# A forward and backward pass of four layers on one core: direct weight transposes, and layer inputs and query pairs transposed by DMA

## The chip, the cores and the metric

The kernel runs on one core of a Trainium2 chip. The engines named here are TensorE (PE, with PEld for its weight loads), VectorE (DVE), ScalarE (ACT), GpSimd (POOL) and SyncE (SP, which issues nearly all DMAs, in its program order). The metric is the device time of one execution, in microseconds (us); the kernel before was timed in three runs.

## The reference

A sequence of 2048 rows of width 512 passes through four residual layers: linear attention A, gated unit B, A, B, with the same weights in both A layers and in both B layers. The kernel returns the output and the gradients with respect to the input and the five weight matrices, all in bf16.

```
def A(x):    # 32 heads of 16, phi(t) = where(t > 0, t + 1, exp(t)) + 1e-6
    q, k, v = heads(x @ wqkv);  pq, pk = phi(q), phi(k)
    kv = pk^T v  (per head);    z = sum over the rows of pk
    return ((pq kv) / (pq . z + 1e-6)) @ wo
def B(x):    # F = 1376
    return (sigmoid(x @ w_gate) * (x @ w_up)) @ w_down
x = x + A(layernorm(x));  x = x + B(layernorm(x))
x = x + A(layernorm(x));  x = x + B(layernorm(x))
out, vjp = jax.vjp(...);  grads = vjp(grad_out)
```

## The kernel before, in words

The 2048 rows are 16 tiles of 128 rows (index `st`, `NST` = 16). The layers are numbered `l` = 0 (A), 1 (B), 2 (A), 3 (B). F = 1376 is taken in three slices (512, 512, 352) and in 11 chunks of 128, the last of which has 96 rows (`FLAST`).

The stages, in order: `kq_fwd` of layer 0 (keys and queries of all tiles, to 60 us); `ab_fwd` of layers 0 and 1 (60 to 205 us), which is called the lower pass here; `kq_fwd` of layer 2 (to 255); `ab_fwd` of layers 2 and 3 (to 395), the upper pass; then the backward pass, `b_bwd_p1` of layer 3, `a_bwd_p1` of layer 2, `b_bwd_p1` of layer 1, `a_bwd_p1` of layer 0. Units of weight gradient (`W.run(n)`, L1495 and L1511) are run between the steps of the backward pass and by themselves where the next step has nothing to do yet; `HOLD` = 6 of them are kept back for the start of `b_bwd_p1` of layer 1.

In these stages PE, ACT, DVE and POOL run in the order in which the program is written. The order of the DMAs on SP is found by the scheduler; `tc.issue_after(x)` only says that a DMA comes after `x`. At most eight DMAs of the queue are under way; each waits for the one issued eight before it.

One tile of an `ab_fwd` pass does the attention part of a tile ahead and the gated unit of tile `st`:

- the "front" of a tile ahead, `FLAG` = 3 tiles: `prod` (POOL, L840), `front1` (DVE, the sum over a head, L846), `front2` (DVE, add and reciprocal L850 and L851, and the multiplication that gives the normalised queries `pqn`, L863), and `front3` (four PE transposes of 128 x 128 to `pqnT`, L374, copied out by ACT);
- `attn_y` of tile `st + 2` (`YLAG`): four matmuls (L884), the residual added on DVE (L892), and the statistics of the next layernorm (DVE and POOL, L449 to L455); `ln.apply` (ACT, L460) makes the normalised input `hstage`, and `ln.stage_T` transposes it to `hT` with four PE transposes (L374) and an ACT copy (L383);
- `gu` for the three slices: g and u products on PE (L922), sigmoids on ACT (L924, L926), `hh_t` on DVE (L929, which releases the bank of u) and `ssd_t` on POOL (L930). PSUM has two banks each for g and u and one for y;
- `hh_t` transposed to `hhT`, by DMA in tiles 2 to 14 (`dma_T`, L949), and `finish` (11 matmuls with w_down, L956) of an earlier tile; tile 3 has no `finish`, so it is shorter. In the lower pass the statistics of the following layernorm come on DVE too.

The backward pass of B needs the three B weights transposed: `wdT`, `wuT`, `wgT`. `wT_units` makes them in the lower pass, piece by piece: a DMA transpose from the input into a staging tile (L404, L406, L420) and a store to DRAM (L409, L412, L421). From there they are loaded whole (L201, L206, L208): in the upper pass after tiles 2, 5 and 8, and by `load_b_weights` at the start of `b_bwd_p1` of layer 1. Of the last chunk of `wuT` and `wgT` only 96 rows are loaded; the transposes of `dd` and the matmuls of `dh` (L1252) take 96 rows there.

`kq_fwd` of layer 0 takes its tiles `a_t` from three buffers; each is stored (`sv_phq`, L642) before it is used again.

Of the kernel before, what the change touches and what calls it, by code (L numbers as in the profile page):

```python
# [60 lines left out]
def kernel(  # L61
# [42 lines left out]
    for l in range(4):  # L104
# [17 lines left out]
    k.wT = dict(  # L122
        wgT=dram.tile([NFC * P, D], BF16, name="wgT_d"),
        wuT=dram.tile([NFC * P, D], BF16, name="wuT_d"),
        wdT=dram.tile([D, F], BF16, name="wdT_d"),
    )
# [12 lines left out]
    with tc.tile_pool(name="wfwd", bufs=1, reuse_waits="tile") as wfwd, ExitStack() as lctx, tc.manual_schedule(engines=EM):  # L139
# [44 lines left out]
        with tc.tile_pool(name="aq0", bufs=1, reuse_waits="tile") as aq:  # L184
            A = kq_fwd(k, aq, 0, lns[0], lns[1], x_bf)
            with tc.tile_pool(name="wt_stage", bufs=2, reuse_waits="tile") as wt_stage:
                piece, flush = wT_units(k, wt_stage, B_w_gate, B_w_up, B_w_down)
                piece()
                piece()
                A.tail()  # L190
                ab_fwd(k, A, lns[1], {**{st: piece for st in range(0, 14, 2)}, NST - 2: flush}, nxt=lns[2])
        xctx.close()
        with tc.tile_pool(name="aq2", bufs=1, reuse_waits="tile") as aq:
# [4 lines left out]
            def b_weight_loads():  # L198
                def wd():
                    k.wdT = wb.tile([P, NDC, F], BF16, name="wdT", tag="w_c")  # L200
                    nc.sync.dma_start(out=k.wdT[:], in_=k.wT["wdT"].rearrange("(c p) f -> p c f", p=P))  # L201

                def wx(nm, tag):
                    t = wb.tile([P, NFC, D], BF16, name=nm, tag=tag)
                    setattr(k, nm, t)
                    nc.sync.dma_start(out=t[:, 0:NFC - 1, :],  # L206
                                      in_=k.wT[nm][0:(NFC - 1) * P, :].rearrange("(c p) j -> p c j", p=P))
                    nc.sync.dma_start(out=t[0:FLAST, NFC - 1, :], in_=k.wT[nm][(NFC - 1) * P:F, :])  # L208
                return wd, lambda: wx("wuT", "w_a"), lambda: wx("wgT", "w_b")
# [20 lines left out]
            def last_cb(i):  # L230
                if i == 0:
                    k.pre["gT"] = pre.tile([P, NDC, P], BF16, name="pre_gT")
                    g_transposes(k, k.pre["g"][:, 0, :], k.pre["gT"])
                else:
                    k.pre["dd"] = pre.tile([P, 2, F], BF16, name="pre_dd")
                    for fs in range(2):
                        dd_ops(k, k.pre["dd"], k.pre["ssd"], fs, dhh_mm(k, k.pre["gT"], fs))
            A.tail()
            ab_fwd(k, A, lns[3], dict(zip((2, 5, 8), b_weight_loads())), out_cb=out_cb, last_cb=last_cb)
# [5 lines left out]
    if True:  # L245
        def load_b_weights():
            wd, wu, wg = b_weight_loads()
            wd()
            wu()
            with tc.issue_after(k.hold):  # L250
                wg()
# [10 lines left out]
        k.load_b_weights, k.load_a_weights = load_b_weights, load_a_weights  # L262
# [55 lines left out]
        a_bwd_p1(k, R, 2, W, mk_out_cb=mk_gbf_cb)  # L318
        W.run(W.left() - HOLD)
# [76 lines left out]
def wT_units(k, stage, B_w_gate, B_w_up, B_w_down):  # L396
    nc = k.nc
    units, stores = [], []

    def by_rows(src, c0, n, dst):  # L400
        def unit():
            t = stage.tile([P, NDC, D], BF16, name="wt_st")
            nfull = min(n, F // P - c0) if src.shape[-1] == F else n
            nc.sync.dma_start(out=t[:, 0:nfull, :], in_=src[:, c0 * P:(c0 + nfull) * P], transpose=True)  # L404
            if nfull < n:
                nc.sync.dma_start(out=t[:, nfull, :], in_=src[:, F - P:F], transpose=True)  # L406

            def store():
                nc.sync.dma_start(out=dst[c0 * P:(c0 + nfull) * P, :].rearrange("(n p) d -> p n d", p=P),  # L409
                                  in_=t[:, 0:nfull, :])  # L410
                if nfull < n:
                    nc.sync.dma_start(out=dst[(c0 + nfull) * P:F, :], in_=t[P - FLAST:P, nfull, :])  # L412
            stores.append(store)
        return unit

    def by_cols(src, f0, w, dst):
        def unit():
            t = stage.tile([P, NDC, D], BF16, name="wt_st")
            v = t[:].rearrange("p a b -> p (a b)")[:, 0:NDC * w].rearrange("p (a b) -> p a b", a=NDC)
            nc.sync.dma_start(out=v, in_=src[f0:f0 + w, :], transpose=True)  # L420
            stores.append(lambda: nc.sync.dma_start(  # L421
                out=dst.rearrange("(c p) f -> p c f", p=P)[:, :, f0:f0 + w], in_=v))
        return unit

    for f0, w in FSL:
        units.append(by_cols(B_w_down, f0, w, k.wT["wdT"]))
    for src, nm in ((B_w_up, "wuT"), (B_w_gate, "wgT")):
        for c0, n in ((0, 4), (4, 4), (8, 3)):
            units.append(by_rows(src, c0, n, k.wT[nm]))

    def flush():
        for store in stores:
            store()
        stores.clear()

    def piece():
        old = stores[:]
        stores.clear()
        units.pop(0)()
        for store in old:  # L440
            store()
    return piece, flush


# [18 lines left out]
class FwdLN:  # L463
# [25 lines left out]
    def stage_T(self, st, evac="vector"):  # L489
# [6 lines left out]
        self.hTs[st] = hT  # L496

# [59 lines left out]
def kq_fwd(k, aq, l, ln, ln_next, x_src=None):  # L557
# [10 lines left out]
    with ExitStack() as ctx:  # L568
# [91 lines left out]
        def qa_tiles():  # L660
            if l == 0:
                return (work.tile([P, 2, D], BF16, name="e_t", bufs=2)[:, 1, :],
                        work.tile([P, 2, D], BF16, name="a_t", bufs=3)[:, 1, :])
# [30 lines left out]
        for st in range(NST):  # L694
# [4 lines left out]
            if l == 0:  # L699
                e_t = work.tile([P, 2, D], BF16, name="e_t", bufs=2)  # L700
                a_t = work.tile([P, 2, D], BF16, name="a_t", bufs=3)
# [123 lines left out]
YLAG = 2  # L825
FP = NFC * P
HH_DMA = {1: range(2, NST - 1), 3: range(2, NST - 1)}


def attn_fronts(k, A, pool, small):  # L830
# [23 lines left out]
    def front2(st):  # L854
# [11 lines left out]
        if st % 2 == 1:  # L866
            nc.sync.dma_start(out=dram_batch(sva["pqn"], st // 2, 2), in_=cur["pqn"][:])

    def front3(st, bank="ln", evac="scalar"):
        if st >= NST:  # L870
            return
        f = F_[st]
        pqnT = pool.tile([P, NDC, P], BF16, name="pqnT", bufs=3)
# [29 lines left out]
def ab_fwd(k, A, ln, side, nxt=None, out_cb=None, last_cb=None):  # L903
# [3 lines left out]
    with ExitStack() as ctx:  # L907
# [4 lines left out]

        by_dma = HH_DMA[l]

# [59 lines left out]
        for st in range(NST):  # L974
# [6 lines left out]
            if st in by_dma:  # L981
                nc.gpsimd.memset(T["hh"][:, F:FP], 0.0)
                A.front1(st + FLAG)
                A.front2(st + FLAG)
                gu(T, hT, 0)
                A.attn_y(st + YLAG)
                A.prod(st + 1 + FLAG)
# [4 lines left out]
                ln.stage_T(st + 1, "scalar")  # L992
                gu(T, hT, 2)
            elif st == 0:
# [40 lines left out]
            if st > 0:  # L1035
                ln.apply(st + YLAG)
                if st == 1:
# [116 lines left out]
def b_bwd_p1(k, l, W, mid):  # L1154
# [3 lines left out]
    if not first:  # L1158
        k.load_b_weights()
    with ExitStack() as ctx:  # L1160
# [39 lines left out]
        def transposes(T, fs):  # L1200
            dd, ddT = T["dd"], T["ddT"]
            fcs = fchunks_of_slice(fs)
            nfull = len([fc for fc in fcs if fc_rows(fc) == P])
            tps = ps_tile(k, "t", [P, 2, 4, P], BF16, "T_ps")
            for a in range(2):
                src = dd_part(dd, a, fs)
                for i, fc in enumerate(fcs):
                    r = fc_rows(fc)
                    nc.tensor.transpose(tps[0:r, a, i, :], src[:, i * P:i * P + r], k.ident[:])  # L1209
            out = ddT[:, 2 * fcs[0]:2 * (fcs[-1] + 1), :].rearrange("p (a n) t -> p a n t", a=2)  # L1210
            nc.scalar.copy(out[:, :, 0:nfull, :], tps[:, :, 0:nfull, :])  # L1211
            if nfull < len(fcs):
                nc.scalar.copy(out[0:FLAST, :, nfull, :], tps[0:FLAST, :, nfull, :])
# [32 lines left out]
        def dh_mm(T, lo, hi):  # L1246
            if lo == 0:
                T["dh"] = ps_tile(k, "y", [P, D], F32, "dh_ps")
            for i in range(lo, hi):
                a, fc = divmod(i, NFC)  # L1250
                r = fc_rows(fc)
                nc.tensor.matmul(T["dh"][:], lhsT=T["ddT"][0:r, dd_block(a, fc), :], rhs=(k.wuT, k.wgT)[a][0:r, fc, :],  # L1252
# [653 lines left out]
```

## Time and profile before

| | us |
|---|---|
| median of 3 runs | 1133.44 (1133.23 to 1135.18) |
| the profiled execution | 1135.02 |
| its span, from the first to the last instruction | 1133.3 |
| PE busy in the span | 1109.4 |
| DVE, ACT, POOL busy | 706.9, 484.2, 291.2 |
| PE busy in the lower pass, 60 to 205 us | 138.5 of 145 |
| PE busy in the upper pass, 255 to 395 us | 134.8 of 140 |

A busy time is the time in which an engine had an instruction under way. A timeline line gives the start, the time taken, the engine, the line of the kernel, the operation, the tile written and the tiles read, and in brackets how long the engine had been idle and what ended that. For a DMA, "to landing" is the time from the start of its issue on SP to its arrival. The DMA share is the mean busy share of the 16 DMA engines; packets that overlap in one engine can bring it over 1.

### The profile page before, as it was taken

Reading aid. Unit: us, or ns where it says so; the run is one execution under the profiler, and the core shown is the slowest. Engines: PE = TensorE matmul, PEld = TensorE weight load, DVE = VectorE, ACT = ScalarE, POOL = GpSimd, SP = SyncE. Lnnn points to the kernel's source line nnn. Section 1 sums busy time; section 2 is a strip of 40 time slices with the busy share of each in tenths; the row PEclk is TensorE's granted clock in tenths of the full one; section 3 lists DMA queues with packets and bytes.
Section 4 is the critical chain, followed back from the end, with each engine's and each line's share of the span. In section 5 each row is a group of like instructions: output and inputs, shape, how many; then the busy total and the mean of one; then the engine's idle time right before and its main releaser. Section 6 shows DMA issues by size and latency. Waiting matters only on the chain.

```text
span 1133.3 us, 20011 instructions
## 1 busy us (share of the span) xinstructions
PE 1109.4 (98%) x7468; PEld 648.8 (57%) x7468; DVE 706.9 (62%) x1344; ACT 484.2 (43%) x909; POOL 291.2 (26%) x518
## 2 busy tenths in 40 slices
PE   8979999998999999999999999999999999999998
PEld 4444554444555555554456468855546745448888
DVE  6788886778776456664975850166664976852211
ACT  6676666555756543433625431224324515410000
POOL 5647776435666400000110220000000110210000
PEclk9999999999999999999999999999999999999999
DMA  8967999855899999997899997799998899969996
GB/s 270 309 197 212 273 282 283 245 142 183 223 294 265 269 261 262 302 255 207 222 244 313 220 260 237 195 283 289 257 283 260 205 282 289 241 194 298 263 205 192
DMA packets 413682, 282.36 MB, mean 249 GB/s; under 512 B 198608, under 2 KB 399504, under 8 KB 409744
## 3 DMA queue, kind: packets, MB, share of 16 engines
q1 hardware_dynamic: 412432, 280.03, 90.3%
q8 instruction: 58, 0.95, 0.3%
q10 hardware_dynamic: 1152, 1.05, 0.3%
q14 instruction: 40, 0.33, 0.1%
HBM read 125.44 MB, written 115.70 MB: 213 GB/s over the span
## 4 chain that ended last, share of the span: by engine, by line
PE 89%; DVE 6%; DMA 3%; ACT 1%; issue 1%; POOL 0%; DVEq 0%; SPq 0%; POOLq 0%
PE p_ps L1511 18%; PE dh_ps L1252 13%; PE dh_ps L1756 7%; PE p_ps L1495 7%; PE y_ps L956 6%; PE dhh_ps L1110 6%; PE g_ps L922 6%; PE u_ps L922 6%; PE T_ps L1209 3%; PE dpk_ps L1791 2%; PE GT_ps L1652 2%; PE dp_ps L1624 2%; PE y_ps L884 2%; PE t_mm L616 2%; PE X_ps L624 2%; PE t_ps L374 1%
## 5 line engine op out<-in xcount | busy, mean ns | idle before, releaser
L1511 PE MATMUL p_ps<-p_set,p_a 128*128 128x256 bf16 (+1 forms) x2032 | 210.1, 264 | 0.0
L1511 PEld LDWEIGHTS <-p_a 128*128 128x128 bf16 x2048 | 185.9, 98 | 22.2
L1132 DVE TENSOR_TENSOR dd<-dhh_ps,ssd 128x512 bf16<-128x512 f32 x144 | 82.4, 629 | 121.3 <-PE dhh_ps L1110 117.4
L930 POOL TENSOR_TENSOR ssd_t<-hh_t,oms 128x512 bf16<-128x512 bf16 (+1 forms) x96 | 100.7, 1060 | 50.1 <-ACT out_t L226 13.5
L1252 PEld LDWEIGHTS <-ddT 128*128 128x128 bf16 (+1 forms) x704 | 67.6, 98 | 74.6 <-DMA ddT<-dd 2.4
L922 PEld LDWEIGHTS <-hT 128*128 128x128 bf16 x768 | 72.5, 98 | 65.2 <-DVE hT L381 1.4
L1084 POOL TENSOR_SCALAR ab<-c 128x2 f32<-128x2 f32 x64 | 12.4, 194 | 377.9 <-DVE junk L1081 364.7
L1211 ACT COPY ddT<-T_ps 128x1024 bf16<-128x1024 bf16 (+1 forms) x72 | 58.8, 819 | 115.2 <-PE T_ps L1209 62.0
L1076 ACT ACTIVATE t_sb<-dh_ps,rstd_all 128x512 f32<-128x512 f32 x64 | 44.0, 688 | 115.7 <-issue 65.0
L922 PE MATMUL g_ps<-wg,hT 128*128 128x512 bf16 (+1 forms) x384 | 90.0, 357 | 0.4 <-DVE hT L381 0.4
L924 ACT ACTIVATE ssd_t<-g_ps 128x512 bf16<-128x512 f32 (+1 forms) x96 | 53.4, 556 | 86.1 <-PE g_ps L922 80.3
L922 PE MATMUL u_ps<-wu,hT 128*128 128x512 bf16 (+1 forms) x384 | 90.0, 357 | 0.0
L1485 DVE TENSOR_TENSOR dw_stg<-p_ps,dw_stg 128x512 bf16<-128x512 f32 (+3 forms) x43 | 28.1, 653 | 98.1 <-PE p_ps L1511 81.4
L929 DVE TENSOR_TENSOR hh_t<-u_ps,ssd_t 128x512 bf16<-128x512 f32 (+1 forms) x96 | 60.4, 631 | 44.0 <-PE u_ps L922 34.2
L1252 PE MATMUL dh_ps<-wgT,ddT 128*128 128x512 bf16 (+1 forms) x352 | 85.2, 379 | 0.0
L1252 PE MATMUL dh_ps<-wuT,ddT 128*128 128x512 bf16 (+1 forms) x352 | 81.3, 379 | 0.8 <-DMA ddT<-dd 0.7
L956 PE MATMUL y_ps<-wd,hhT 128*128 128x512 bf16 (+1 forms) x352 | 81.3, 379 | 0.6 <-DVE x L958 0.6
L1495 PE MATMUL p_ps<-p_a,p_set 128*128 128x512 bf16 (+1 forms) x352 | 81.2, 379 | 0.0
L1110 PE MATMUL dhh_ps<-wdT,gTb 128*128 128x512 bf16 x336 | 74.2, 357 | 0.0
L956 PEld LDWEIGHTS <-hhT 128*128 128x128 bf16 (+1 forms) x352 | 34.2, 98 | 41.1 <-issue 0.7
L1081 DVE SCALAR_TENSOR_TENSOR junk<-t_sb,h_ld 128x512 bf16<-128x512 f32 x48 | 37.2, 774 | 28.9 <-ACT t_sb L1076 23.7
L926 ACT ACTIVATE oms<-g_ps 128x512 bf16<-128x512 f32 (+1 forms) x96 | 52.8, 550 | 3.9 <-POOL ssd_t L930 3.7
(227 smaller groups left out, 1824.2 us busy)
## 6 DMA issues: line engine op xcount, KB each, us to landing
p_set<-sv_hdd SPq DMA_DIRECT2D x30, 1024.0 KB, 6.2
sv_ssd<-ssd_t SPq DMA_DIRECT2D x32, 688.0 KB, 4.2
ssd<-sv_ssd SPq DMA_DIRECT2D x24, 688.0 KB, 5.1
sv_hdd<-dd SPq DMA_DIRECT2D x24, 512.0 KB, 5.0
sv_hdd<-hh_t SPq DMA_DIRECT2D x32, 320.0 KB, 4.4
p_a<-sv_h SPq DMA_DIRECT2D x16, 512.0 KB, 6.5
p_set<-sv_dqk SPq DMA_DIRECT2D x8, 1024.0 KB, 7.5
h_ld<-sv_h SPq DMA_DIRECT2D x24, 256.0 KB, 4.7
```

Of the source, the lines that this page charges most:

```text
L922: nc.tensor.matmul(ps[:, 0:w], lhsT=hT[:, kc, :], rhs=w_sb[:, kc, c0:c0 + w], start=(kc == 0), stop=(kc == NDC - 1))
L924: nc.scalar.activation(ssd_t[:, 0, c0:c0 + w], g_ps[:, 0:w], ACT.Sigmoid)
L929: nc.vector.tensor_tensor(hh_t[:, c0:c0 + w], u_ps[:, 0:w], ssd_t[:, 0, c0:c0 + w], ALU.mult)
L930: nc.gpsimd.tensor_tensor(ssd_t[:, 1, c0:c0 + w], hh_t[:, c0:c0 + w], oms[:, 0:w], ALU.mult)
L956: nc.tensor.matmul(y_ps[:], lhsT=T["hhT"][0:r, fc, :], rhs=k.wd[0:r, fc, :], start=(fc == 0), stop=(fc == NFC - 1))
L1110: k.nc.tensor.matmul(ps[:, 0:w], lhsT=gT[:, jc, :], rhs=k.wdT[:, jc, c0:c0 + w], start=(jc == 0), stop=(jc == NDC - 1))
L1132: k.nc.vector.tensor_tensor(dd_part(dd, a, fs), ps[:, 0:w], ssd[:, a, c0:c0 + w], ALU.mult)
L1211: nc.scalar.copy(out[:, :, 0:nfull, :], tps[:, :, 0:nfull, :])
L1252: nc.tensor.matmul(T["dh"][:], lhsT=T["ddT"][0:r, dd_block(a, fc), :], rhs=(k.wuT, k.wgT)[a][0:r, fc, :], start=(i == 0), stop=(i == 2 * N ...
L1495: nc.tensor.matmul(ps[0:r, :], lhsT=set_t[:, st, c * P:c * P + r], rhs=self.ops[j["l"], "g"][:, st, :], start=(st == 0), stop=(st == NST - 1))
L1511: nc.tensor.matmul(ps[:, icl * w:(icl + 1) * w], lhsT=self.ops[j["l"], "h"][:, st, ic * P:(ic + 1) * P], rhs=set_t[:, st, 0:w], start=(st ...
L1756: nc.tensor.matmul(dh_ps[:], lhsT=lhsT, rhs=rhs, start=(i == 0), stop=(i == len(ops) - 1))
```

## The change

It has four parts.

- Weights. `wT_units` and the DRAM copies are gone. Each B weight is transposed by DMA from the input straight into its place, in pieces: in the upper pass four pieces ahead of `A.tail()` and five more after tiles 0, 1 and 2; for layer 1 the three of `wgT` after `k.hold`, and those of `wdT` and `wuT` one after every three units of weight gradient, ahead of `W.run(W.left() - HOLD)` instead of at the start of `b_bwd_p1`.
- The last chunk. It is loaded as the last 128 rows, and 32 of them are set to zero by POOL (`zero_rows`), so that `dd` transposes, their copies and the `dh` matmuls take 128 rows throughout.
- Layer input. In both passes `hT` of tiles 3 to 15 is made by a DMA transpose of `hstage` (`dma_T`), issued right after `ln.apply`, in place of four PE transposes and an ACT copy.
- Queries, lower pass only. From tile 3 on the front runs one tile further ahead (`ahead` = `st` + 4), at the top of the tile. `pqn` of tiles 6 to 15 is transposed by DMA, two tiles at a time (`pqT`), in `front2` of the odd tile; `front3` is left out for them. Tile 3 does `front2` of tiles 6 and 7.

`a_t` in `kq_fwd` of layer 0 has four buffers in place of three. The order of PE's instructions in the backward pass stays as it was.

```diff
-    def by_rows(src, c0, n, dst):
-            nc.sync.dma_start(out=t[:, 0:nfull, :], in_=src[:, c0 * P:(c0 + nfull) * P], transpose=True)
...
-                nc.sync.dma_start(out=dst[c0 * P:(c0 + nfull) * P, :].rearrange("(n p) d -> p n d", p=P),
-                                  in_=t[:, 0:nfull, :])
...
-            with tc.tile_pool(name="wt_stage", bufs=2, reuse_waits="tile") as wt_stage:
-                piece, flush = wT_units(k, wt_stage, B_w_gate, B_w_up, B_w_down)
-                piece()
-                piece()
-                A.tail()
-                ab_fwd(k, A, lns[1], {**{st: piece for st in range(0, 14, 2)}, NST - 2: flush}, nxt=lns[2])
+            A.tail()
+            ab_fwd(k, A, lns[1], {}, nxt=lns[2])
...
+                def by_cols(f0, w):
+                    def load():
+                        if f0 == 0:
+                            tiles["wdT"] = k.wdT = wb.tile([P, NDC, F], BF16, name="wdT", tag="w_c")
+                        return nc.sync.dma_start(out=tiles["wdT"][:, :, f0:f0 + w], in_=B_w_down[f0:f0 + w, :],
+                                                 transpose=True)
...
+                def by_rows(src, nm, tag, c0, n):
...
+                        ins = nc.sync.dma_start(out=t[:, c0:c0 + n, :], in_=src[:, c0 * P:(c0 + n) * P], transpose=True)
+                        if c0 + n == NFC - 1:
+                            ins = nc.sync.dma_start(out=t[:, NFC - 1, :], in_=src[:, F - P:F], transpose=True)
...
+                def zero_rows():
+                    for nm in ("wuT", "wgT"):
+                        nc.gpsimd.memset(tiles[nm][0:P - FLAST, NFC - 1, :], 0.0)
+                parts = [(0, 4), (4, 3), (7, 3)]
...
+            pieces = sum(b_weight_loads(), [])
+            def some():
+                for _ in range(2):
+                    if pieces:
+                        pieces.pop(0)()
+            some()
+            some()
             A.tail()
-            ab_fwd(k, A, lns[3], dict(zip((2, 5, 8), b_weight_loads())), out_cb=out_cb, last_cb=last_cb)
+            ab_fwd(k, A, lns[3], {**{st: some for st in range(3)}, NST // 2: k.zero_rows}, out_cb=out_cb,
+                   last_cb=last_cb)
...
         def load_b_weights():
             wd, wu, wg = b_weight_loads()
-            wd()
-            wu()
             with tc.issue_after(k.hold):
-                wg()
+                for ld in wg:
+                    ld()
+            for pair in zip(wd, wu):
+                for ld in pair:
+                    W.run(3)
+                    with tc.issue_after(k.last_set):
+                        ld()
...
         a_bwd_p1(k, R, 2, W, mk_out_cb=mk_gbf_cb)
+        load_b_weights()
         W.run(W.left() - HOLD)
...
+    def dma_T(self, st):
+        if st >= NST:
+            return
+        self.hTs[st] = hT = self.k.lnres["hT"].tile([P, NDC, P], BF16, name="hT")
+        self.k.nc.sync.dma_start(out=hT[:], in_=self.hs.pop(st), transpose=True)
...
-                        work.tile([P, 2, D], BF16, name="a_t", bufs=3)[:, 1, :])
+                        work.tile([P, 2, D], BF16, name="a_t", bufs=4)[:, 1, :])
...
+PQ_PE = {0: 5, 2: NST}
+HT_DMA = range(3, NST)
...
         if st % 2 == 1:
+            if st > PQ_PE[A.l]:
+                pqT = A.wide.tile([P, 2 * NDC, P], BF16, name="pqT")
+                nc.sync.dma_start(out=pqT[:], in_=cur["pqn"][:].rearrange("p n d -> p (n d)"), transpose=True)
+                for i in range(2):
+                    F_[st - 1 + i]["T"] = pqT[:, i * NDC:(i + 1) * NDC, :]
             nc.sync.dma_start(out=dram_batch(sva["pqn"], st // 2, 2), in_=cur["pqn"][:])
     def front3(st, bank="ln", evac="scalar"):
-        if st >= NST:
+        if st > PQ_PE[A.l] or st >= NST:
             return
...
+        more = l == 1
...
-                A.front1(st + FLAG)
-                A.front2(st + FLAG)
+                ahead = st + FLAG + (more and st > 2)
+                if more and st == 3:
+                    A.front2(st + FLAG)
+                A.front1(ahead)
+                A.front2(ahead)
                 gu(T, hT, 0)
                 A.attn_y(st + YLAG)
-                A.prod(st + 1 + FLAG)
+                A.prod(ahead + 1)
...
-                ln.stage_T(st + 1, "scalar")
+                if st + 1 not in HT_DMA:
+                    ln.stage_T(st + 1, "scalar")
                 gu(T, hT, 2)
+                if more and st == 2:
+                    A.prod(ahead + 2)
+                    A.front1(ahead + 1)
+                    A.rden(ahead + 1)
...
                 ln.apply(st + YLAG)
+                if st + YLAG in HT_DMA:
+                    ln.dma_T(st + YLAG)
...
-                    nc.tensor.transpose(tps[0:r, a, i, :], src[:, i * P:i * P + r], k.ident[:])
+                for i in range(n):
+                    e = min((i + 1) * P, w)
+                    nc.tensor.transpose(tps[:, a, i, :], src[:, e - P:e], k.ident[:])
```

## The prediction

> **What bounds the kernel now.** I read, in this order, the head of the page (busy time by engine), the busy time by window of the two forward passes, the waits, and the timelines of the lower pass, tile by tile. TensorE (PE) bounds nearly everywhere:
>
> ```profile
> PE 1109.4 (98%) x7468; PEld 648.8 (57%) x7468; DVE 706.9 (62%) x1344; ACT 484.2 (43%) x909; POOL 291.2 (26%) x518
> ...
> q1 hardware_dynamic: 412432, 280.03, 90.3%
> ```
>
> So an instruction taken off PE is worth its PE time, if nothing else is late in its place. How near the others are is read from the windows. The first line is tiles 5 to 11 of the lower pass, the second eight tiles of the upper pass; the columns are the window, its length, PE, PEld, DVE, ACT and POOL busy (instructions), granted clock, DMA share, GB/s:
>
> ```profile
> 110.25:168.62 58.37, 58.37 (x333) 29.82 (x331) 51.70 (x91) 38.39 (x71) 45.35 (x79) 1.00 1.05 276
> 301.00:367.60 66.60, 66.60 (x379) 33.98 (x377) 48.42 (x88) 41.53 (x81) 42.59 (x65) 1.00 0.98 282
> ...
> 667.00:731.00 64.00, 64.00 (x624) 57.55 (x623) 4.32 (x8) 12.13 (x22) 3.07 (x6) 1.00 0.75 218
> ```
>
> In the lower pass a tile takes 58.37/7 = 8.34 us, all of it PE, while VectorE (DVE) is busy 89% and the DMA engines are full. In the upper pass DVE is at 73%. The third line is the stretch of weight-gradient units ahead of the second backward GLU layer: PE full, DVE nearly idle, DMA not full.
>
> **The PE transposes leave: -8.0 us.** They stand in the PE timeline of the lower pass, four at a time, between the `gu` groups of g and u products; those of `hstage` give `hT`, those of `pqnstage` give `pqnT`:
>
> ```profile
> 141.94 0.39 PE L374 MATMUL ln_tp<-ident,hstage 128*128 128x128 bf16 x4
> 142.16 0.76 PE L922 MATMUL g_ps<-wg,hT 128*128 128x352 bf16 x4
> ```
>
> From the start of four to the start of the next group is 0.22 us (the 0.39 of the line contains the last one's latency, which is overlapped). The change drops 13 groups for `hT` in each pass and 10 for `pqnT` in the lower one: 36 x 0.223 = 8.0 us, 5.1 of it in the lower pass and 2.9 in the upper. The 36 ACT copies (0.586 us each) that go with them are off the path, ACT being busy 66%: nothing.
>
> **The fourth `a_t` buffer: -1.7 us.** In the first projection stage DVE waits for a store to release an `a_t` buffer, and PE waits for DVE behind it:
>
> ```profile
> 47.25 0.49 DVE L636 TENSOR_SCALAR a_t<-e_t 128x512 bf16<-128x512 bf16 x1 [2.71 <-DMA sv_phq<-a_t]
> ...
> 48.52 1.02 PE L616 MATMUL y_mm<-wqkv,hTst 128*128 128x512 bf16 x4 [1.73 <-DVE pk_all L639]
> ```
>
> With four buffers the store waited for is one tile older (a tile there is about 2.7 to 3.5 us), so the 2.71 us fall to nothing or near it, and PE's 1.73 us go. The next late thing is ACT's `e_t`, which these lines show ready before. Bounds: 0 and 1.73; I take 1.73.
>
> **Two fronts in tile 3 of the lower pass: +2.7 us.** The normalised queries are now formed one tile earlier, so at tiles 2/3 DVE makes tile 6 and tile 7 before it may evacuate `gu` slice 0 (L929 `hh_t`). Tile 3 is the short one (no `finish`): before, it starts at 95.71 and its first `hh_t` at 98.69, 2.98 in.
>
> ```profile
> 96.25 1.96 POOL L930 TENSOR_TENSOR ssd_t<-hh_t,oms 128x512 bf16<-128x512 bf16 x2
> ...
> 98.69 0.68 DVE L929 TENSOR_TENSOR hh_t<-u_ps,ssd_t 128x512 bf16<-128x512 f32 x1
> ```
>
> The new POOL product for tile 7 (1.16 us, L840) runs behind those two `ssd_t`, to 2.50 + 1.16 = 3.66 into the tile; then DVE's reduce 0.71, add 0.21, reciprocal 0.39, multiply 0.82: the first `hh_t` starts at 5.8 and ends at 6.5. PE wants that bank for `u` of slice 2 at 1.73 + 0.86 + 1.73 + 0.60 = 4.9: 1.6 us of stall. Behind it DVE needs 0.71 + 0.73 + 0.1 + 0.67 before slice 1 is evacuated, 8.7, and tile 4, starting at 7.1, wants that bank at 7.9: 0.8 us. Tile 4 is as late at its end, by the same count: 0.5. Sum 2.9, less the 0.2 us that PE now waits at 103.4. Bounds: 0, if the slack in the banks takes it, and 4.5, if a fourth tile stalls.
>
> **Transfers that PE now waits for.** In the lower pass the bytes balance: per two tiles a 512 KB weight transpose and a 512 KB store leave, two `hT` (128 KB) and one `pqT` (256 KB) come; SP's issue time too, 2.64 + 0.58 us a piece against three issues of some 1.25 (L404/L406 rows). The nearest row to the new transfers is `hhT`, in this pass:
>
> ```profile
> L949 SPq DMA_TRANSPOSE hhT<-hh_t x13: 1407/1842/2610, 96.3 to 193.8; - x13
> ...
> DMA to landing us min/median/max: 3.8/4.5/6.7
> ```
>
> `hT` of tile t+2: its input (ACT L460) ends 0.90 into tile t+1, `hhT` goes ahead of it on SP at 0.6 for 1.84, so it is issued at 2.45 and lands at 6.9; the new tile ends at 7.89. Nothing, from +0 (3.8) to 1.3 us a tile (6.7). `pqT`: SP reaches it behind `hhT`, `hT`, `ssd`, `hdd` and `hdl`, at 5.3 in the odd tiles; PE wants it 1.73 into the next, at 9.62. 5.3 + 4.5 = 9.8: 0.2 us x 5 = +1.0 (0 at 3.8; 12 at 6.7). In the upper pass `hT` of tile 4 has the short tile 3 to land: issued at 2.0, landing 4.0 to 4.2, wanted at 5.74: +0.5. There `hT` of tile 5 stands behind the last two weight pieces, issued some 3.7 into tile 4, wanted 8.1: +0.3 (0 to 4.9, by the longest `hhT` of that pass, 9.3). The other weight pieces of that pass are issued between 250 and 289, where the DMA share of before is 0.34 to 0.49.
>
> The Trainium skill (Advanced Engine Details and Errata, X-Bar Transpose (TRN2)) says that transpose DMAs on trn2 are as fast as regular ones. The trace doesn't agree for these small ones: `hhT`, 352 KB, lands in 4.5 us where `sv_ssd`, 688 KB, lands in 4.2. By that rule the 0.5 and the 0.3 would go, and the sum would be -6.0.
>
> **At nothing.** The backward weights now transposed: wdT and wuT land between 672 and 705, in the third window above, and are used at 731; wgT lengthens SP's queue by some 8 us at 658, where the next `h_ld` feeds DVE work that PE doesn't need for 60 us. PE's own order of the backward half is unchanged. The 32 zeroed rows: four memsets of 0.13 us on POOL, one behind a weight's landing, with only `gb_t` and `ab` behind it, at the same place. `dd` transposes of 128 columns for 96, one ACT copy (about 0.8 us) for two (0.58 + 0.37): same PE count.
>
> **Sum.** The profiled execution took 1135.0 us (span 1133.3 and 1.7 around it): -8.0 - 1.7 + 2.7 + 1.0 + 0.5 + 0.3 = -5.2, 1129.8. The median of the runs is 1.6 below that execution: 1133.4 - 5.2 = **1128.2**.
>
> **Rivals.** *All of it hidden*: no stall in tiles 3 to 5, all transfers in time: -9.7, 1123.7. For it: before, PE waits for a DMA in these passes nowhere. Against it: the count for tile 3 uses only durations in the rows.
>
> *DVE and POOL hold the lower pass.* They form a loop of their own:
>
> ```profile
> 144.51 1.96 POOL L930 TENSOR_TENSOR ssd_t<-hh_t,oms 128x512 bf16<-128x512 bf16 x2
> ...
> 144.78 0.92 DVE L850 TENSOR_SCALAR den<-den 128x32 f32<-128x32 f32 x1
> ...
> 152.91 1.96 POOL L930 TENSOR_TENSOR ssd_t<-hh_t,oms 128x512 bf16<-128x512 bf16 x2
> ...
> 153.12 0.99 DVE L850 TENSOR_SCALAR den<-den 128x32 f32<-128x32 f32 x1
> ```
>
> It returns every 8.40 us, not every 8.34, and L850 grows from 0.72 to 1.12 over tiles 6 to 12: it waits for the first `ssd_t` to end, which depends on the `hh_t` behind L850. At a PE tile of 7.89 that loop would bind: 9 tiles x 0.51 = 4.6 us, 1132.8. Against it: L850 starts 1.20 into the tile and `ssd_t` 5.97 after the first `hh_t`; once that lags by over 3.12, L850 goes first (0.18, as in tile 5) and the next turn takes 7.6. So I take it as a brake that lets go. The Trainium skill (SBUF — State Buffer, SBUF: two separate sides) calls the port pair of VectorE and GpSimd an exclusive lock held for the whole instruction; L850's 0.18 against 0.92 agrees.
>
> *`hT` lands too late, slower than before.* It decides at a landing 5.4 us after issue (7.89 - 2.45). At 5.9, within `hhT`'s range, each of some 12 lower tiles loses 0.46 and 11 upper ones 0.24: +8.2, 1136.4; at 6.7, over 1145. For it: DMA full, one SP queue, no slack but a tile. Against it: the median 4.5, and a third of `hhT`'s bytes.
>
> **How the numbers follow.** The forecast 0.45, all hidden 0.15, the loop 0.20, late `hT` 0.20. 0.2% is 2.3 us, about what a measurement of this kernel can tell from no change: the first two lie beyond it (faster 0.60), the loop within (same 0.20), the last beyond on the other side (slower 0.20). The range runs from 1124, nearly all hidden, to 1137, half of the late case; the forecast's own is 1126 to 1131.
>
> **What would show it.** Right: tiles 5 to 12 of the lower pass at 7.9 us and of the upper at 8.11; no PE wait near 48.5; waits of PE on DVE `hh_t` near 100 to 106; `pqT` landings some 4.5 us. Wrong: lower tiles at 8.3 or 8.4 with L850 long in each; PE waiting on `hT` or `pqT` tile after tile; a PE gap near 731, if the backward weights are late.

## The result, and the profile after

The changed kernel is slower: 1142.79 us median of 7 runs (1138.87 to 1146.49), against 1134.76 for the kernel before in the same comparison (1133.23 to 1139.23). The ratio is 1.0072, 95% interval [1.0058, 1.0086]. The forecast, 1128.2 on 1133.4, was a ratio of 0.995. The profiled execution took 1145.07 us, its span 1143.3; before it was 1135.02.

The head of the page of the changed kernel, answering to that of before:

```profile
PE 1105.2 (97%) x7324; PEld 641.0 (56%) x7324; DVE 705.3 (62%) x1344; ACT 462.5 (40%) x841; POOL 292.9 (26%) x522
...
q1 hardware_dynamic: 437824, 276.36, 90.9%
```

PE has 144 matmul records fewer and is busy for 4.2 us less, in a span that is 10 us longer: its idle time went from 23.9 to 38.1 us. (The forecast took 8.0 us of transposes off PE. Of the difference, 0.7 us lies at 193 to 261 us, where the granted clock fell to 0.57 for a few us; the rest was not taken apart.) The busy time by window, for seven tiles of the lower pass (5 to 11), eight of the upper (5 to 12) and the stretch of weight-gradient units (window, length, PE, PEld, DVE, ACT, POOL, granted clock, DMA share, GB/s):

```profile
109.80:168.50 58.70, 55.89 (x275) 26.40 (x273) 52.25 (x94) 30.89 (x58) 47.51 (x81) 1.00 0.98 253
301.70:367.80 66.10, 65.32 (x349) 32.24 (x347) 50.62 (x90) 37.25 (x73) 44.91 (x69) 1.00 0.96 257
668.80:736.60 67.80, 64.81 (x631) 57.58 (x630) 4.31 (x8) 12.12 (x22) 4.63 (x9) 1.00 0.94 230
```

Before, PE was busy for the whole of all three. Now it is idle for 2.8, 0.8 and 3.0 us in them. The PE timeline of the changed kernel names the waits of the lower pass, in brackets:

```profile
100.65 0.76 PE L912 MATMUL u_ps<-wu,hT 128*128 128x352 bf16 x4 [1.90 <-DVE hh_t L919]
102.78 1.02 PE L912 MATMUL u_ps<-wu,hT 128*128 128x512 bf16 x4 [0.51 <-DVE hh_t L919]
111.36 1.02 PE L912 MATMUL u_ps<-wu,hT 128*128 128x512 bf16 x4 [0.53 <-DVE hh_t L919]
121.66 1.04 PE L872 MATMUL y_ps<-M_sb,pqT 128*128 128x512 bf16 x4 [1.39 <-DMA pqT<-pqnstage]
138.43 1.04 PE L872 MATMUL y_ps<-M_sb,pqT 128*128 128x512 bf16 x4 [0.82 <-DMA pqT<-pqnstage]
172.22 1.04 PE L872 MATMUL y_ps<-M_sb,pqT 128*128 128x512 bf16 x4 [1.82 <-DMA pqT<-pqnstage]
```

and those of the weight-gradient stretch:

```profile
695.91 14.15 PE L1508 MATMUL p_ps<-p_set,p_a 128*128 128x256 bf16 x128 [0.55 <-DMA p_set<-sv_hdd]
711.38 7.16 PE L1508 MATMUL p_ps<-p_set,p_a 128*128 128x256 bf16 x64 [1.33 <-DMA p_set<-sv_hdd]
719.65 15.51 PE L1508 MATMUL p_ps<-p_set,p_a 128*128 128x256 bf16 x160 [1.10 <-DMA p_set<-sv_hdd]
```

To see where 10 us went, I cut the PE timeline of each profiled execution at the same instructions: the first g product of each pass and of its tile 15, the first and last `dhh` group of each backward GLU layer, the last `dh` group of each backward attention layer. The lengths in us, with the forecast's share; the right-hand columns are the experiments below ("P first" has `pqT` ahead of the stores, "no Q" leaves out the part on the queries). The last row ends with PE's last group, some 3 us before the end of the span.

| stretch | forecast | before | after | after, again | W alone | P first | no Q | mended |
|---|---|---|---|---|---|---|---|---|
| to the lower pass | -1.7 | 68.4 | 66.6 | 67.8 | 67.3 | 67.2 | 67.5 | 67.4 |
| lower pass, tiles 0 to 14 | -1.4 | 123.9 | 126.8 | 125.9 | 123.4 | 122.6 | 121.2 | 124.9 |
| to the upper pass | 0 | 67.1 | 67.7 | 67.5 | 67.6 | 67.1 | 67.0 | 67.0 |
| upper pass, tiles 0 to 14 | -2.1 | 123.6 | 122.9 | 124.1 | 123.1 | 123.8 | 123.9 | 123.4 |
| its tile 15 | 0 | 10.2 | 10.3 | 10.3 | 10.2 | 10.3 | 11.8 | 10.5 |
| first backward GLU layer | 0 | 123.4 | 123.3 | 123.3 | 123.3 | 123.3 | 123.3 | 123.1 |
| backward attention | 0 | 150.3 | 151.2 | 149.8 | 149.8 | 150.1 | 149.7 | 149.7 |
| weight-gradient stretch | 0 | 64.3 | 67.8 | 67.6 | 67.2 | 66.2 | 67.4 | 64.3 |
| second backward GLU layer | 0 | 122.7 | 125.1 | 124.0 | 122.6 | 123.0 | 124.0 | 124.8 |
| last backward attention | 0 | 150.2 | 152.4 | 149.9 | 150.9 | 150.1 | 149.9 | 150.2 |
| rest | 0 | 125.9 | 125.9 | 125.9 | 126.3 | 125.9 | 125.9 | 125.9 |

Two stretches lost what the forecast did not have, in both executions of the change: the lower pass, 4.3 and 3.4 us over the forecast, and the weight-gradient stretch, 3.5 and 3.3. The upper pass gave 1.4 less than forecast in the first and 2.6 less in the second. The other 4.6 us of the two later backward layers are mostly scatter of one execution: in the second, 1.0 was left. Up to some 1.5 us in the rows around the start of a pass is chance too. Ahead of each pass PE waits 1.6 and 1.2 us, before and after the change, and in every trace but that of before the granted clock then fell, to 0.50 or little above, for a few us at the start of one pass or of both. It need not come from the change: 19 of 26 runs of the kernel before, in the comparison of the copy experiment below, have a mean clock of 0.997 as well, the other seven 1.000.

### The profile page after: what moved, and what is told of

Read it like the earlier page. It is cut to its first block, busy times and chain, and to the rows that moved or that the text cites. A ratio compares the mean times of both kernels' runs of the same rounds, so it can differ in the third digit from the quotient of the medians.

```text
span 1143.3 us, 19700 instructions
## 1 busy us (share of the span) xinstructions
PE 1105.2 (97%) x7324; PEld 641.0 (56%) x7324; DVE 705.3 (62%) x1344; ACT 462.5 (40%) x841; POOL 292.9 (26%) x522
## 5 line engine op out<-in xcount | busy, mean ns | idle before, releaser
L1132 DVE TENSOR_TENSOR dd<-dhh_ps,ssd 128x512 bf16<-128x512 f32 x144 | 82.4, 628 | 124.1 <-PE dhh_ps L1110 123.0
L1211 ACT COPY ddT<-T_ps 128x1024 bf16<-128x1024 bf16 (+1 forms) x72 | 65.5, 913 | 118.5 <-PE T_ps L1209 65.2
L1249 PEld LDWEIGHTS <-ddT 128*128 128x128 bf16 x704 | 67.6, 98 | 77.1 <-DMA ddT<-dd 4.9
L1249 PE MATMUL dh_ps<-wgT,ddT 128*128 128x512 bf16 x352 | 85.1, 379 | 0.0
L1249 PE MATMUL dh_ps<-wuT,ddT 128*128 128x512 bf16 x352 | 81.2, 379 | 3.1 <-DMA ddT<-dd 3.1
L916 ACT ACTIVATE oms<-g_ps 128x512 bf16<-128x512 f32 (+1 forms) x96 | 52.7, 549 | 10.6 <-POOL ssd_t L920 10.5
```

Source lines behind the costliest of these rows:

```text
L916: nc.scalar.activation(oms[:, 0:w], g_ps[:, 0:w], ACT.Sigmoid, scale=-1.0)
L1132: k.nc.vector.tensor_tensor(dd_part(dd, a, fs), ps[:, 0:w], ssd[:, a, c0:c0 + w], ALU.mult)
L1211: nc.scalar.copy(out, tps[:, :, 0:n, :])
L1249: nc.tensor.matmul(T["dh"][:], lhsT=T["ddT"][:, dd_block(a, fc), :], rhs=(k.wuT, k.wgT)[a][:, fc, :], start=(i == 0), stop=(i == 2 * NFC - 1))
```

## The experiments

Letters in the table: W is the weights part (with the zeroed rows), H the layer inputs by DMA, Q the queries. All of them have the fourth `a_t` buffer and, like the changed kernel itself, two buffers in place of three for PE's own `pqnT`; the description of the change doesn't name that last edit, and the run of the `a_t` buffer alone, which has it too, is not slower.

### One part at a time, and W undone

W alone is the changed kernel with

```
-PQ_PE = {0: 5, 2: NST}
-HT_DMA = range(3, NST)
+PQ_PE = {0: NST, 2: NST}
+HT_DMA = ()
-        more = l == 1
+        more = False
```

H alone, Q alone, and H with Q have the weights as before (`wT_units`, DRAM copies).

> The weights part alone (direct transposes, zeroed rows) and the fourth a_t buffer, the layer inputs and queries as before. Theory A (the loss sits in the backward half, where the big weight transposes hold up SP and the loads of p_set): the trace of after gains 4.7 us between 655 and 735 and 2.5 more at 843, so 1134.8 - 1.8 + 5 to 7 = 1138 to 1140. Theory B (the loss is the late pqT and hT of the forward passes; what came later in the backward half is scatter of that one execution): 1134.8 - 1.8 = 1133, with no wait of PE on p_set above 0.5 us.

> The layer inputs by DMA alone (tiles 3 to 15 of both passes) and the fourth a_t buffer; weights by way of DRAM and queries on PE as before. 26 groups of four transposes at 0.223 us are 5.8 us. Theory A (only the weights cost): 1134.8 - 1.8 - 5.8 = 1127 to 1128. Theory B (transposes land late where the DMA engines are full, and here the lower pass keeps the weight pieces): 1130 to 1135, with waits of PE on hT in several tiles of the lower pass.

> The queries alone (two fronts in tile 3, pqT in pairs) and the fourth a_t buffer; layer inputs on PE and weights by way of DRAM as before. 10 groups at 0.223 us leave, 2.2 us; the two fronts cost 2.7. Theory A: 1134.8 - 1.8 - 2.2 + 2.7 + 1.0 = 1134.5. Theory B (pqT stands on SP behind hhT and the three stores of the tile before and lands 1 to 2 us late in each even tile): 1134.8 - 1.8 - 2.2 + 2.7 + 5 to 9 = 1138 to 1142, the weight pieces making it worse than in after.

> Everything of the change but the weights part, which is as before. Theory A (the weights cost 7 us or more in the backward half): 1131 to 1135, and the time after 400 us is that of before within 1 us. Theory B (the forward passes cost): 1138 to 1143, the lower pass 3 us or more longer than before's 145.

| kernel | median us | ratio | 95% | lower pass, profiled |
|---|---|---|---|---|
| W alone | 1140.79 | 1.0042 | [1.0026, 1.0057] | 123.4 |
| H alone | 1151.88 | 1.0146 | [1.0131, 1.0161] | 133.6 |
| Q alone | 1160.51 | 1.0226 | [1.0197, 1.0256] | 149.0 |
| H and Q | 1176.09 | 1.036 | [1.0341, 1.038] | 157.2 |

Both theories were too simple. Theory A is right that W costs, and the trace of W alone has its price where that theory put it: 67.2 us for the weight-gradient stretch, 2.9 more than before. But H and Q with the old weights are far worse than with the new: H made the lower pass 9.7 us longer, Q 25.1. So W pays for the other parts. The SP queue of Q alone shows how, ahead of the `pqT` that PE waits for at 148.91 (the last line is PE's):

```profile
138.50 1.14 SPq L1081 DMA_DIRECT2D sv_hdl<-hh_t  x1
139.69 1.93 SPq L404 DMA_TRANSPOSE wt_st<-in_B_w_up_dram  x1
141.66 1.25 SPq L406 DMA_TRANSPOSE wt_st<-in_B_w_up_dram  x1
142.96 0.58 SPq L409 DMA_DIRECT2D wuT_d<-wt_st  x1
143.64 1.75 SPq L877 DMA_TRANSPOSE pqT<-pqnstage  x1
...
148.91 1.89 PE L897 MATMUL y_ps<-M_sb,pqT 128*128 128x512 bf16 x4 [4.03 <-DMA pqT<-pqnstage]
```

The weight piece of that tile stands in front of `pqT` and keeps SP for 3.95 us. The flights of `pqT` are not what differs: their median is 4.0 us here and 3.7 in the changed kernel. Of theory B, the first half holds (the late transposes are a loss of the forward passes), and its second half falls: the W stretch is no scatter.

The executions of W alone lie at 1136.96 (the profiled one) and 1140.4 to 1141.0 (four others). Its trace so explains 1.9 of the 5.8 us; what the others lost was not seen.

### `pqT` ahead of the stores

```
+                while held:
+                    with tc.issue_after(k.pqT_ins):
+                        held.pop(0)()
...
+            if more and st in (4, 6, 8, 10):
+                held.append(stores)      # ssd, hdd and hdl of this tile
```

> The changed kernel with one order changed on SP: the three stores of tiles 4, 6, 8 and 10 of the lower pass are issued behind pqT instead of ahead of it. Theory P (pqT lands late because SP reaches it only 6.1 to 8.1 us into the odd tile; its flight of 3.7 us is as forecast): pqT is issued some 2.2 us earlier, the waits of PE on pqT (4.8 us together at tiles 6, 8, 10, 12) go, the lower pass falls from 126.8 to 122 or 123 us, the time by 4 to 5 to about 1138. Rival F (the DMA engines are full, so that pqT lands late wherever it stands on SP): flights grow to 6 us, the pass stays within 1.5 us of 126.8.

Measured: 1138.47 us, ratio 1.0037 [1.002, 1.0053], where the change has 1.0072; the lower pass 122.6. The SP queue of tile 5 in the changed kernel (the tile starts at 109.8; the columns are start, time on SP, line):

```profile
111.80 2.49 SPq L939 DMA_TRANSPOSE hhT<-hh_t  x1
114.39 1.21 SPq L477 DMA_TRANSPOSE hT<-hstage  x1
115.69 0.54 SPq L1053 DMA_DIRECT2D sv_ssd<-ssd_t  x1
116.28 0.42 SPq L1054 DMA_DIRECT2D sv_hdd<-hh_t  x1
116.76 1.04 SPq L1056 DMA_DIRECT2D sv_hdl<-hh_t  x1
117.90 1.89 SPq L852 DMA_TRANSPOSE pqT<-pqnstage  x1
```

and in this one:

```profile
111.86 2.33 SPq L940 DMA_TRANSPOSE hhT<-hh_t  x1
114.28 1.21 SPq L477 DMA_TRANSPOSE hT<-hstage  x1
115.59 1.26 SPq L852 DMA_TRANSPOSE pqT<-pqnstage  x1
```

On its PE timeline the product of tile 6 follows the one before it with no gap, where the changed kernel waited 1.39 us:

```profile
119.31 1.03 PE L913 MATMUL u_ps<-wu,hT 128*128 128x512 bf16 x4
120.17 1.03 PE L873 MATMUL y_ps<-M_sb,pqT 128*128 128x512 bf16 x4
```

`pqT` goes out 2.3 us earlier and every PE wait on it is gone (one of 0.9 us on an `hT` has come). Tiles 7 to 13 follow one another at 7.88 to 7.90 us, and the pass takes 122.6 us, where the forecast had 122.5. Theory P holds, rival F falls: the median flight is 3.2 us here and was 3.7 there.

### Q undone, and layer 1's weights from a DRAM copy

No Q is the changed kernel with the two Q lines of the first diff. The copy is

```
+            if st in (2, 4, 6):          # in the first backward GLU layer
+                k.copy_out(("wdT", "wuT", "wgT")[st // 2 - 1])
...
-        load_b_weights()
         W.run(W.left() - HOLD)
...
-        k.zero_rows()
+        k.load_b_weights()               # three plain loads
```

> The changed kernel without its part on the queries: fronts three tiles ahead and pqn transposed on PE throughout. Theory P with the count of the traces: the two fronts in tile 3 (2.9 us of PE waits) and the late pqT (4.8) go, ten groups of four transposes come back (2.2): the lower pass at 126.8 - 5.5 = 121.3, the time about 1137.5. Rival L (the loop of DVE and POOL, 8.40 us a tile, holds the lower pass): tiles 5 to 12 at 8.3 to 8.4 instead of 8.11, the pass at 123.5, the time about 1139.5.

Measured: 1137.41 us, ratio 1.0012 [0.9998, 1.0027], the lower pass 121.2. Theory P's count was 121.3. Here is the busy time by window of tiles 5 to 11 of no Q:

```profile
108.56:165.33 56.77, 56.77 (x304) 28.21 (x302) 51.61 (x92) 34.12 (x64) 46.28 (x78) 1.00 0.90 238
```

and its `den` adds on the DVE timeline, in tiles 5 to 8:

```profile
109.76 0.20 DVE L833 TENSOR_SCALAR den<-den 128x32 f32<-128x32 f32 x1
117.87 1.16 DVE L833 TENSOR_SCALAR den<-den 128x32 f32<-128x32 f32 x1
125.98 0.18 DVE L833 TENSOR_SCALAR den<-den 128x32 f32<-128x32 f32 x1
134.09 0.94 DVE L833 TENSOR_SCALAR den<-den 128x32 f32<-128x32 f32 x1
```

PE is full at 8.11 us a tile, below the 8.40 of the DVE and POOL loop. A short add comes back after one long one, and after two behind these lines (0.18, 0.70, 1.00, 0.18); the adds stand 8.11 us apart throughout. So the loop lets go when it lags, as the forecast had argued, and rival L falls. The kernel with `pqT` ahead of the stores says the same at 7.89 us a tile: its adds in tiles 5 to 11 take 0.18 to 0.25 us but for one of 1.17.

> The changed kernel, but layer 1 gets its three backward weights by plain loads from a DRAM copy at the start of its backward layer, as the kernel before does; the copy is stored from SBUF during the first backward GLU layer. Theory W (the transposes of the weights in the stretch of weight-gradient units hold SP for 5 to 7 us each, so that the p_set loads go out late): the stretch falls from 67.8 to 64.3 us, the end of the layer before it by up to 1.5, the time by 4 to 5 to about 1138, with no PE wait on p_set. Rival S (the 3 us of p_set waits are scatter): no change beyond 1 us, 1142 to 1143; or the three stores slow the first backward layer (123.3 us) by 1 to 3.

Measured: 1142.98 us, ratio 1.0065 [1.0045, 1.0085]. The stretch went to 64.3 us with no wait on `p_set`, as theory W has it; but the first backward GLU layer went from 123.3 to 126.4, which fits the clause on the three stores. The waits of PE in that layer, none of them there in the changed kernel:

```profile
PE dh_ps L1256 <- DMA ddT<-pre_dd: 1.7, 2, 1.4
PE dhh_ps L1117 <- DVE pre_dd L1139: 0.8, 1, 0.8
```

> The changed kernel without the part on the queries and with layer 1's weights loaded from the DRAM copy: both edits together. If both losses are as the traces put them, 1142.8 - 5.5 - 4.4 = 1133, and 1.5 less where the second backward GLU layer runs in 122.7 us and not 125.1: level with the kernel before or up to 0.3% faster. If the loop of DVE and POOL holds the lower pass, 1135; if the stores of the copy collide with the first backward layer, 1136.

Measured: 1139.68 us, ratio 1.004 [1.0027, 1.0052]: the stretch 64.3, the first backward GLU layer 129.1, with PE waits of 2.3 and 1.5 us and a granted clock of 0.50 to 0.67 at 412 to 416. A missed hope: that layer, with a DMA share of 0.95 in the changed kernel and 1.02 here, gives back more than the gain. That the stores do it is likely, not shown: of the traced kernels without them, one (the four upper tiles on PE, below) had 125.3 us there too, with a wait of 1.8 us on `ddT`.

### The `a_t` buffer alone, the upper pass, smaller pieces, and the change again

The buffer alone is the kernel before with `bufs=4`. The upper pass puts four tiles back on PE, on top of no Q:

```
-HT_DMA = range(3, NST)
+HT_DMA = {1: range(3, NST), 3: (3, *range(6, NST - 2))}
```

and the smaller pieces, on top of that, are wdT in six column blocks of 256 and wuT in five pairs of chunks, spread wider:

```
-            for pair in zip(wd, wu):
-                for ld in pair:
-                    W.run(3)
+            small = [*wd[0:2], wu[0], *wd[2:4], wu[1], *wd[4:6], *wu[2:5]]
+            for i, ld in enumerate(small):
+                W.run(3 if i < 6 else 2)
```

> The kernel before with the fourth a_t buffer alone (and two pqnT buffers in place of three, to make room). By the trace of after, where PE reaches the point near 48 us 1.9 us earlier and keeps 1.8 of it to 96 us: 1135.1 - 1.8 = 1133.3, 0.2% faster. Rival: the gain is given back where the input and weight transfers of the first pass become late: within 0.5 us of before.

> The changed kernel without the queries part, and with the upper pass's hT of tiles 4, 5, 14 and 15 on PE again. Theory H (in the upper pass hT lands late behind the weight pieces in tiles 3 to 5 and behind the last stores in tile 14, 1.65, 0.65 and 0.3 us): that pass falls from 123.9 to 121.8 us, the time from 1137.4 to about 1135. Rival (the waits move to the next tiles): 123 to 124 us, 1137.

> The changed kernel without the queries part, with the upper pass's hT of tiles 4, 5, 14 and 15 on PE again, and with layer 1's wdT and wuT in eleven smaller pieces spread over 28 units of weight gradient in place of six over 18. Theory W (a piece holds SP for up to 7 us and the p_set loads go out late behind it; not the bytes): no PE wait on p_set, that stretch at 64.5 us in place of 67.4, 2.5 to 3 us faster than the kernel with the same passes and six pieces: 1132. Rival (the bytes of the transposes in the full DMA engines are what delays p_set): the waits stay at 2 to 3 us, 1134.5.

> The changed kernel once more, for the scatter between its executions. If the 125.1 us of the second backward GLU layer and the 152.4 of the last backward attention layer belong to the change, they return; if they are scatter of that one execution, they come to 122.7 to 124 and 150 to 151, while the lower pass (126.8) and the stretch of weight-gradient units (67.8) stay within 0.7 us.

The buffer alone: 1133.60 us, ratio 0.9987 [0.9977, 0.9996], as expected. The upper pass with four tiles back: 121.4 us in place of 123.9, by theory H, with no wait on `hT`; but 1138.97 us, ratio 1.0034 [1.002, 1.0047]: the weight-gradient stretch of that kernel was at 69.3 us with 4.1 us of waits on `p_set`, and its first backward GLU layer at 125.3. The 121.4 did not come back, either: the two later kernels with the same upper pass had 122.9 us, with a wait of 0.64 us on the `hT` of tile 6, and 123.4. So the rival holds in part: waits in the tiles behind stayed or came back. The smaller pieces: 64.3 us for the stretch and 1133.60, 1.6 us above what was expected, ratio 0.9992 [0.9982, 1.0003]. The change again: 1141.07, its stretches in the table.

The SP queue in the stretch, first of the changed kernel, then with the smaller pieces:

```profile
689.95 6.52 SPq L196 DMA_TRANSPOSE wdT<-in_B_w_down_dram  x1
696.56 0.53 SPq L1360 DMA_DIRECT2D p_set<-sv_hdd  x1
...
697.62 4.92 SPq L206 DMA_TRANSPOSE wuT<-in_B_w_up_dram  x1
702.59 1.61 SPq L196 DMA_TRANSPOSE wdT<-in_B_w_down_dram  x1
704.30 0.53 SPq L1360 DMA_DIRECT2D p_set<-sv_hdd  x1
```

```profile
677.19 0.84 SPq L1361 DMA_DIRECT2D p_set<-sv_hdd  x1
...
678.56 3.99 SPq L206 DMA_TRANSPOSE wuT<-in_B_w_up_dram  x1
682.65 0.53 SPq L1361 DMA_DIRECT2D p_set<-sv_hdd  x1
...
692.20 2.25 SPq L206 DMA_TRANSPOSE wuT<-in_B_w_up_dram  x1
694.68 0.40 SPq L1361 DMA_DIRECT2D p_set<-sv_hdd  x1
```

Before, a `p_set` was issued every 7.0 us, when its buffer came free. With big pieces the `p_set` waits on SP until they are out, and the load issued at 704.30 is, by its landing, the one that PE waits for until 711.38. With the smaller ones the bytes are the same and no PE wait on `p_set` is left in the stretch, while the DMA engines are fuller and not emptier: a share of 1.00 and 243 GB/s over 64.3 us, against 0.94 and 230 over 67.8. The flights of `p_set` hardly differ (median 6.3 us, 7.0 with big pieces, 6.1 before). So it is SP's time and its spacing, not the bytes. Size and spacing were changed together, so which of the two does it stays open.

### The whole change, with its three losses mended

The last two kernels: the whole change with `pqT` ahead of the stores, the smaller pieces, and the four upper tiles on PE; and the kernel of the smaller pieces with the upper pass wholly on PE (`3: ()`).

> The whole change, with the three losses that the runs have shown mended and nothing else: stores of tiles 4, 6, 8 and 10 behind pqT (4.2 us in the lower pass), wdT and wuT in eleven pieces over 28 units (3.3 to 3.5 us), hT of tiles 4, 5, 14 and 15 of the upper pass on PE (1 to 2 us). If these three are the whole difference between the forecast and the result, the time is 1142.5 - 4.2 - 3.4 - 1.5 = 1133.4, and what is left against before is the two fronts of tile 3 (2.9 us) against the gains. If something is still unnamed, for instance in the late ddT of the second backward GLU layer (122.7 us before, 124.0 and 125.1 in the two executions of the changed kernel), it stays at 1136 or more.

> The changed kernel without the queries part, the weights of layer 1 in eleven pieces, and hT by DMA in the lower pass only, the upper pass wholly on PE. If hT by DMA is worth something in the upper pass where only tiles 3 and 6 to 13 have it (9 groups, 2.0 us, less the late tile 3), this is 1 to 1.5 us slower than the kernel that differs from it in that alone: 1135. If the transposes there cost what they save: the same 1133.6 within 0.6.

Mended: 1134.59 us, where before was at 1136.33 in that comparison; ratio 0.9979 [0.9965, 0.9993]. That is 1.7 us below before, as expected, and by the two ratios 0.92%, some 10.5 us (2 either way), below the change as made, where the three mends were counted at 9.1. So together they bring back what the change had lost, and this version is ahead of the kernel before by little.

The traced execution bears this out in full for the weight-gradient stretch only (64.3 us). Its lower pass, at 124.9, did not reach 122.6: PE waits 1.5 us for two `hT`, and tile 0 took 9.30 us (8.32 before) with the granted clock at 0.50 to 0.69 from 66 to 72. Its upper pass, at 123.4, is within the scatter. The waits of PE in its two forward passes no longer name `pqT`; both of the waits on `hT` are in the lower one:

```profile
PE u_ps L914 <- DVE hh_t L921: 2.9, 3, 1.9
...
PE g_ps L914 <- DMA hT<-hstage: 1.5, 2, 0.9
```

The upper pass wholly on PE: 1135.06, ratio 0.9993 [0.9978, 1.0007], against 0.9992 with `hT` by DMA in nine of its tiles. So these transposes save nothing measurable there; the traces (124.6 us wholly on PE, 122.9 and 123.4 with nine tiles by DMA) are one execution each.

## Why the prediction was wrong

Two terms failed. `pqT` was put at +1.0 us and cost 4.8, and the backward weights were put at nothing and cost 3.3 to 3.5; both are waits for what stands behind other transfers on SP. Term by term:

- **PE transposes, -8.0.** Right in itself: undisturbed tiles of the lower pass take 7.89 us where they took 8.34, of the upper 8.11.
- **The fourth `a_t` buffer, -1.7.** Right in its mechanism: PE's wait near 48.5 is gone from every trace with the buffer, and the buffer alone is worth 0.13% (1.5 us, 0.5 to 2.6 by its interval). The lower pass starts 1.8 us earlier in the first execution of the change and 0.6 in the second, where the granted clock fell to 0.50 at 66 us.
- **Two fronts in tile 3, +2.7.** Right: 1.90 + 0.51 + 0.53 = 2.94 us, in the places that were named.
- **`pqT`, +1.0.** This step failed by size. Tiles 6, 8, 10 and 12 took 1.56, 0.99, 0.24 and 1.99 us over 7.89, 4.8 in all. The flight was better than priced (a median of 3.7 us, not 4.5; 4.8 ahead of the longest wait). The issue was not at 5.3 us into the odd tile but at 6.1 to 8.1: the last `hh_t` of the tile before ends 0.8 to 1.9 into the tile (with the fronts now ahead of it on DVE), so that `hhT` goes out at 0.9 to 2.0 and not 0.6; `hT` keeps SP for 1.2 to 1.9 us and the three stores for 2.0 to 2.3. Each was some tenths over the row that I had taken, and there was no slack: the stated bounds (0 and 12 us) held it, the value between them was too low.
- **`hT` in the lower pass, nothing.** Right once the weight pieces are gone: no wait in the changed kernel. The bytes balance, as the forecast argued, but what mattered was that the pieces leave SP.
- **`hT` of tiles 4 and 5 of the upper pass, +0.8.** By tile lengths 0.27 us for tile 4. The `hT` of tile 5 was in time; what came instead is 1.12 us in tile 5, a wait of 0.34 us for `pqnT` and one of 0.44 for the `hT` of tile 6. Behind both stand waits of DVE, POOL and ACT (1.50, 2.06 and 1.48 us, at 299.0 to 305.4) for the stores `sv_hdl` and `sv_ssd` that give their buffers free. At the other end came an unforeseen 1.14 us wait for `hT` of tile 15, which stood on SP behind the first `gTb` of the backward pass (4.17 us). So the pass gained 0.7 us in the first execution, lost 0.5 in the second, and not 2.1.
- **The backward weights, at nothing.** This step failed by kind. I looked whether the DMA engines had room in the stretch (0.75 before) and whether the weights came in time for 731. They did. What was late were the loads behind them on SP, which I had counted for wgT and not for the six pieces of wdT and wuT: SP is kept 4.9 to 7.3 us by four of them, and the stretch grew by 1.9 to 5.0 us in the traced kernels that have these pieces.
- **Rivals.** "Late `hT`, slower than before" had the right sign and half of the mechanism: one crowded SP queue, but what came late was `pqT` and `p_set`, not `hT`. "The DVE and POOL loop" is refuted by 8.11 us a tile without Q and by 7.89 with `pqT` ahead of the stores. "All of it hidden" was not: the stall in tile 3 came as counted.
- **The sum.** Forecast -5.2 us, measured +8.0. The mends bring back some 10.5 of these 13 us; the mended kernel is still about 3 us short of the forecast, and the upper pass, where `hT` by DMA gained nothing measurable in place of 2.1, is the largest named part of it.
- **Open.** The second backward GLU layer took 122.5 to 122.7 us in the three traced kernels that have neither H nor Q, and 123.0 to 125.1 in every other, through late `ddT`. SP issues its DMAs there in the same order in the kernels with and without H that I compared, and I have no cause for it.

By the rule of the Trainium skill that was weighed (Advanced Engine Details and Errata, X-Bar Transpose (TRN2)), transpose DMAs cost what regular ones do. This trace disagrees again, in flight (`hhT`, 352 KB, 4.0 us in the lower pass; `sv_ssd`, 688 KB, 3.7) and most of all on SP: 1.2 to 2.1 us for `hT`, 0.5 for the `ssd` store at 115.69.

## What to carry to other kernels

Price a transfer by the time at which its queue reaches it, with everything that is issued ahead of it and each at its own upper row, before its flight; a queue with no slack turns tenths into a wait of the bound engine. A part that takes work off a queue can be what makes the other parts possible, so single parts are measured against the whole. Where big transposes share a queue with loads that must go out on time, make them small and spread them.

## What the runs showed of the hardware

A wait of PE on a transfer can cost much more than its length. In Q alone PE waits 4.03 us for `pqT`; the eleven matmuls behind it then take 4.67 us for 2.54. The windows of 2 us around it, with the granted clock in the third column from the end:

```profile
146.00:148.00 2.00, 0.00 (x0) 0.00 (x0) 1.03 (x2) 0.41 (x1) 0.83 (x1) 1.00 1.30 121
148.00:150.00 2.00, 1.08 (x3) 0.43 (x4) 0.00 (x0) 0.00 (x0) 0.32 (x1) 0.52 1.21 320
150.00:152.00 2.00, 2.00 (x6) 0.73 (x5) 1.13 (x2) 0.00 (x0) 0.00 (x0) 0.50 1.04 385
152.00:154.00 2.00, 2.00 (x6) 0.63 (x5) 0.44 (x2) 0.00 (x0) 1.24 (x4) 0.50 0.55 164
154.00:156.00 2.00, 2.00 (x9) 0.84 (x8) 0.69 (x1) 0.00 (x0) 0.92 (x1) 0.78 0.00 0
```

All five waits on `pqT` of that pass (2.37 to 4.03 us) were followed by a clock of 0.50 to 0.54, and by `finish` groups of 4.0 to 4.7 us for 2.54. So 14.7 us of waits on `pqT` and 2.0 on `hh_t` could make the lower pass 25.1 us longer. The Trainium skill (TensorE: Matmul & The Clock Gate, Part 1) has the clock fall to half after about 3.4 us of idleness, in windows that run freely. The half rate agrees, 0.50; here less was at times enough: in Q alone a wait of 2.85 us was followed by 0.50, in H alone one of 2.44 by 1.00. The changed kernel's lower pass, with waits of at most 1.9 us, kept 1.00. Two waits close together can do it too: the 1.63 and 1.22 us ahead of the upper pass were followed by 0.57 at 258 to 262 in the same execution, the same two ahead of its lower pass by 1.00.

How long a transpose keeps SP does not follow from its size. A wdT piece of 512 x 512 kept it for 2.25 us at 616 and for 6.52 at 690, in one execution of the changed kernel; a `pqT` 1.26 us with the stores behind it and 1.89 with them ahead. What lengthens it no run here shows.
